# Attention with normalized queries and keys on one core: norm factors as bf16 pairs, query copies added up as 64-bit integers on GpSimd, and a new order of all engines

## The chip, the core and the metric

The kernel runs on one core of a Trainium2 chip. The core has TensorE (matrix products, into PSUM), VectorE, ScalarE and GpSimd (element-wise work), and SyncE, which here issues most DMAs. Each engine works through its own list of instructions in order; semaphores hold an instruction until its inputs are there. The metric is device time in microseconds (us) of one execution. In the profile PE is TensorE, DVE is VectorE, ACT is ScalarE, POOL is GpSimd and SP is SyncE.

## The reference

```python
B, H, S, D = 1, 32, 2048, 640
Dh = D // H          # 20
# q, k, v: [1, 32, 2048, 20] bf16;  t: [32] bf16, 1.0 and a little more
def reference(q, k, v, t):
    eps = 1e-6
    qn = q / (jnp.sqrt((q * q).sum(axis=-1, keepdims=True)) + eps)
    kn = k / (jnp.sqrt((k * k).sum(axis=-1, keepdims=True)) + eps)
    logits = jnp.einsum('bhqd,bhkd->bhqk', qn, kn) * t[None, :, None, None]
    attn = _softmax(logits, axis=-1)
    return jnp.einsum('bhqk,bhkd->bhqd', attn, v)
```

There are 32 heads with 2048 queries and 2048 keys of 20 numbers each. So the products are small and the 32 x 2048 x 2048 exponentials are many. Logits lie within about plus and minus t, so no maximum is subtracted.

## The kernel before, in words

**Preparation.** Heads are prepared in groups of one to four. VectorE squares q and k (L1008), sums over the 20 numbers (L1011), takes the reciprocal root by an integer estimate and a polynomial step (L1015 to L1030, tiles `rs_u`, `rs_a`, `rs_b`, `rs_y`, `rs_r`, all f32), multiplies the factors of the queries by the temperature of the head (L1036, `t_f`), and multiplies q and k by their factors into `qkn`, bf16, 32 columns a row (L1054). Columns 20 to 22 hold constants that make room for offsets in the products. A transposing DMA on SyncE's queue turns `qkn` into `qkT` (L1072): 32 partitions for each of four groups of rows, queries in columns 0 to 511 and keys in 512 to 1023. Six more DMAs make copies of the keys rotated among the partition groups (`kR`), four make copies of the queries with zeros in half of the partitions (`qz`). Head 0 has a shorter way of its own through TensorE (`first_head`).

**Two ways to an exponential.** A head is cut into 16 tiles of (4 x 128 keys) x 512 queries, four units of 128 x 512 each. A tile takes one of two ways.

- *ScalarE's way.* TensorE forms the query products (L1161, or L1168 with `qz`) in waves of two and three units alternately in `psA`, and ScalarE writes the exponential of a wave (1024 or 1536 columns) into `p_ring` (L1267). TensorE's value products of four units follow (L1189, `psF<-p_ring,vaug`).
- *VectorE's way.* TensorE multiplies the keys by `qP`, a copy of the queries in which each partition has been multiplied by a factor of its own (L1064, factors in `pcol`): 1 for the odd groups, 8192 for the even, and special factors on the constants. So one f32 in `psF` carries the logits of two units. VectorE reads a tile of 128 x 1024 out of `psF` as int32 with one multiplication and addition (L1318): each 32-bit word of `xt` is then two 16-bit floats, which approximate two powers of two. Three phase additions make three copies `ss` with an integer added to each word, which moves the kinks of the approximation. The additions of a tile may run on VectorE in a fast form (L1340, or two tiles in one by L1345) or a slow form with gaps in the output (L1338, only the third phase), or on GpSimd as 64-bit integer additions, two words an element, in pieces of any length (L1350). TensorE's value products read `xt` and the three `ss`, the latter with values scaled to the phase (`vph`, L971).

`DVE_TILES` lists how many of the 16 tiles of each head go VectorE's way. The list's sum is 205; ScalarE has the other 307 tiles, which are 1228 units.

**Output.** The value products of a head add up in one bank of `psF`, two banks alternating. VectorE transposes it (L1205), takes the reciprocal of the sums (L1214), multiplies (L1222), and SyncE stores two heads at a time.

**The order.** `Program.list_schedule` plans all engines before anything is issued: a list scheduler in which each task has planned duration, dependences and a due time. ScalarE's and VectorE's product tasks go ahead of value products. Each stretch of 10 us of planned time has its own set of knobs, packed in a number of `STAGES` and unpacked by `turn`. GpSimd gets its pieces in `cont_fill`. It works beside VectorE's "light" tasks (tile reads, slow phase additions, transposes); a piece is planned to begin after the last other ("heavy") VectorE task, and gets a wait on that task. Heavy tasks are the squares, sums, normalizations, query copies, fast phase additions and the like. `plan_waits` then turns dependences into semaphore waits, and `emit` writes each engine's list. Where TensorE would stand idle long, the planner may put in fillers, value products with zero weights (L1094).

The tasks around the change: `add_prep` (norms and normalization), `add_qp` (query copies; they are due 1.5 heads ahead of their head and wait for the transposing DMA of it), `add_trn` (transposes and copies by DMA), `add_wave`, `add_group` and `add_dgroup` (products, exponentials, tile reads and phase additions).

Of the kernel before, what the change touches and what calls it, by code (L numbers as in the profile page):

```python
# [10 lines left out]
BF16 = mybir.dt.bfloat16  # L11
# [42 lines left out]

class Task:
# [3 lines left out]
                 "own", "left")  # L59

    def __init__(self, eng, name, fn, dur, deps, pri, lat=0.0, dma=None):
# [13 lines left out]
        self.own, self.left = None, False  # L75
# [6 lines left out]
class Program:  # L82
# [27 lines left out]
        "WAITH": (0.3, 0.1, 0.6), "BLOG": (5, 3, 4, 7, 9, 99), "PTWO": (1, 0), "STAY": (1, 0), "URGE": (3, 2, 4, 6), "BOOST": (1.0, 0.0, 0.4, 4.0), "DPV": (0.0, 0.3, 0.65, 1.0), "FLIP": (0, 2, 4, 8), "FSOON": (0.3, 0.0, 0.8, 3.0), "JOIN": (0.8, 0.0, 0.4, 1.4), "MERGE": (0.0, 0.2, 0.4), "SLOT": (1, 0), "SPARE": (0.35, 0.25, 0.5)}  # L110
    STAGES = (323660128748544, 350903769007104, 596268605500308, 596320203303492, 596320191857220, 596316966994500, 595491402138182, 595491402132374, 595542999852948, 598645317787860, 598851709001940, 506388444610260, 258353002618204, 258353002618192, 258359452343632, 258359401581952, 258352951607584, 99844499194144, 258352951607728, 311189460894448, 311189460894448, 411357472924204, 411357472920723, 411718657544787, 570227109956499, 570220481072019, 570220481072019, 570220481072019, 543802405669779, 385293952981107, 385293941037173, 384468376180877, 701485281505421, 701485281505409, 701485818747507, 701485818802224, 701485818802224, 701472943240944, 701472943240944, 701472943239216, 859981395652608, 859981397145600, 861013771243971, 543686861512754, 543686861512752, 493378820286042, 652663031351901, 810344306477949, 648540582288375, 14500321833210, 122546067191103, 702972302468002, 24310418509344, 681779003975634, 731275100514633, 324749016460711, 324749016460711, 324749016460711, 324749016460711)
# [42 lines left out]
    def list_schedule(self, until=None):  # L154
# [166 lines left out]
        def cont_fill(now):  # L321

            n = 0
            while free["POOL"] <= now + 1e-9:
# [14 lines left out]
                fit = [r for r in ready["POOL"] if r[2].win]  # L339
                if fit:  # L340
# [3 lines left out]
                    t = x[2]  # L344
                else:
# [1108 lines left out]
```

## Time and profile before

| what | before |
|---|---|
| median of 3 runs | 572.65 us |
| lowest and highest run | 571.52 and 572.72 us |
| span of the profiled execution | 570.9 us |
| TensorE products, busy | 552.1 us (97%), 6257 instructions |
| VectorE, busy | 554.1 us (97%), 669 instructions |
| ScalarE, busy | 558.9 us (98%), 499 instructions |
| GpSimd, busy | 454.9 us (80%), 459 instructions |

The profiled execution's own time is its span, 570.9 us; the times of the runs are device times that also take in what lies around the span, and their median is 1.75 us above it. Busy time is the time in which at least one instruction of an engine has a record open. Records of neighbouring instructions may overlap, so the mean of a group of instructions can be longer than what one more of them costs. A row of the groups gives line, engine, operation, output and input, shapes, count, then busy time, mean of one in ns, and the idle time of the engine just before them with what ended it. A row of the chain of waits or of the timeline gives start, length, and what ran.

### The profile page before, as it was taken

To read this page: it belongs to the slowest core of one execution; us is meant where nothing else is said; L and a number is where in the kernel's file an instruction comes from. 1 tells how busy PE (TensorE), PEld (TensorE's weight loads), DVE (VectorE), ACT (ScalarE), POOL (GpSimd) and SP (SyncE) were. 2 spreads that over 40 slices of the span, in tenths; PEclk is the share of its full clock that TensorE was granted. 3 is DMA by queue.
4 is the path that set the end of the run, shared out by engine and by line. 5 is a ranking of instruction groups with operands and counts; after the bars stand their busy time and mean duration, and the time that the engine had idled before them with its cause. 6 is when DMAs were issued, how large, how long until landed. Compare 5 with 4: busy or idle time off the path is not lost.

```text
span 570.9 us, 15004 instructions
## 1 busy us (share of the span) xinstructions
PE 552.1 (97%) x6257; PEld 151.5 (27%) x6257; DVE 554.1 (97%) x669; ACT 558.9 (98%) x499; POOL 454.9 (80%) x459
## 2 busy tenths in 40 slices
PE   8998999999998999999999999999999999999997
PEld 2222222222222222222222222222222222222222
DVE  8999999999999999999999999999999999999994
ACT  6999999999999999999999999999999999999995
POOL 6476959687796787977989788886888969899873
PEclk9999999999999999999999999999999999999999
DMA  5553444634446433434423433434334322321000
GB/s 69 64 84 71 59 53 96 76 85 45 79 77 71 83 69 66 63 53 75 67 70 56 76 57 64 67 65 75 48 71 73 59 69 48 54 62 40 14 1 18
DMA packets 195763, 35.60 MB, mean 62 GB/s; under 512 B 172272, under 2 KB 195696, under 8 KB 195696
## 3 DMA queue, kind: packets, MB, share of 16 engines
q1 hardware_dynamic: 195552, 34.57, 37.6%
q8 instruction: 49, 0.80, 0.6%
q14 instruction: 18, 0.15, 0.1%
q10 hardware_dynamic: 144, 0.08, 0.1%
HBM read 7.87 MB, written 2.62 MB: 18 GB/s over the span
## 4 chain that ended last, share of the span: by engine, by line
ACT 80%; PE 17%; DMA 1%; DVE 1%; SPq 0%; issue 0%
ACT p_ring L1267 80%; PE psF L1189 10%; PE psA L1161 3%; PE psA L1168 2%; PE psF L1173 1%; DMA qkT<-qkn 1%; PE psF L1087 1%; SPq L844 0%; DVE xt L1318 0%; DVE oT L1205 0%; DVE ones L847 0%; DVE o_stage L1222 0%; PE psA L1121 0%; DVE qkT L1133 0%; DVE qP L1064 0%
## 5 line engine op out<-in xcount | busy, mean ns | idle before, releaser
L1267 ACT ACTIVATE p_ring<-psA 128x1024 bf16<-128x1024 f32 x492 | 555.3, 1458 | 1.6 <-PE psA L1161 1.6
L1350 POOL INT64_ADD ss<-xt x400 | 446.0, 1136 | 106.8 <-DVE qkn L1054 25.5
L1318 DVE TENSOR_SCALAR xt<-psF 128x1024 int32<-128x1024 f32 x205 | 249.1, 1215 | 2.7 <-PE psF L1173 2.3
L1189 PE MATMUL psF<-ss,vph 128*32 128x512 f16 (+1 forms) x2460 | 214.0, 397 | 0.1
L1338 DVE TENSOR_SCALAR ss<-xt 128x1040 int32<-128x1040 int32 x159 | 193.8, 1222 | 0.9 <-PE psF L1189 0.8
L1189 PE MATMUL psF<-p_ring,vaug 128*32 128x512 bf16 x1228 | 114.3, 384 | 0.4 <-DVE xt L1318 0.4
L1161 PE MATMUL psA<-qkT,kR 32*128 32x512 bf16 x655 | 100.5, 385 | 6.3 <-ACT p_ring L1267 5.1
L1189 PE MATMUL psF<-xt,vaug 128*32 128x512 bf16 (+1 forms) x820 | 82.4, 394 | 0.6 <-DVE xt L1318 0.5
L1189 PEld LDWEIGHTS psF<-ss,vph 128*32 128x32 f16 x2460 | 54.6, 94 | 81.0 <-issue 51.9
L1168 PE MATMUL psA<-qz,kR 64*128 64x512 bf16 x313 | 64.6, 386 | 1.6 <-ACT p_ring L1267 1.1
L1173 PE MATMUL psF<-qP,kR 64*128 64x512 bf16 x284 | 54.7, 382 | 1.5 <-DVE xt L1318 1.4
L1161 PEld LDWEIGHTS psA<-qkT,kR 32*128 32x128 bf16 x655 | 24.7, 91 | 100.6 <-ACT p_ring L1267 99.9
L1189 PEld LDWEIGHTS psF<-p_ring,vaug 128*32 128x32 bf16 x1228 | 30.4, 94 | 49.7 <-issue 40.1
L1161 PE MATMUL psA<-qkT 32*128 32x512 bf16 x177 | 35.1, 384 | 3.0 <-ACT p_ring L1267 2.5
L1168 PEld LDWEIGHTS psA<-qz,kR 64*128 64x128 bf16 x313 | 15.8, 92 | 63.6 <-ACT p_ring L1267 62.5
L1205 DVE STREAM_TRANSPOSE oT<-psF 128x512 f32<-128x512 f32 x32 | 22.7, 710 | 6.9 <-PE psF L1189 6.6
L1189 PEld LDWEIGHTS psF<-xt,vaug 128*32 128x32 bf16 x820 | 21.2, 94 | 30.0 <-issue 22.7
L1173 PE MATMUL psF<-qP,qkT 64*128 64x512 bf16 x126 | 24.3, 382 | 0.0
L1054 DVE TENSOR_TENSOR qkn<-qk_sb,rs_r 128x1280 bf16<-128x1280 bf16 (+1 forms) x17 | 23.2, 1362 | 0.0
L1011 DVE TENSOR_REDUCE rs_sum<-sq 128x64 f32<-128x1280 bf16 (+1 forms) x17 | 23.0, 1354 | 0.0
L1173 PEld LDWEIGHTS psF<-qP,kR 64*128 64x128 bf16 x284 | 13.7, 93 | 24.1 <-DVE xt L1318 11.3
L1168 PE MATMUL psA<-qz,qkT 64*128 64x512 bf16 x83 | 19.8, 386 | 0.1
(75 smaller groups left out, 144.0 us busy)
## 6 DMA issues: line engine op xcount, KB each, us to landing
kR<-qkT SPq DMA_DIRECT2D x62, 96.0 KB, 2.2
kR<-qkT SPq DMA_DIRECT2D x62, 64.0 KB, 2.1
qz<-qkT SPq DMA_DIRECT2D x104, 32.0 KB, 1.9
qk_sb<-in_k_dram SPq DMA_DIRECT2D x32, 80.0 KB, 3.0
vaug<-in_v_dram SPq DMA_DIRECT2D x32, 80.0 KB, 3.3
qk_sb<-in_q_dram SPq DMA_DIRECT2D x124, 20.0 KB, 2.5
out_dram<-o_stage SPq DMA_DIRECT2D x31, 80.0 KB, 1.8
kR<-qkT SPq DMA_DIRECT2D x62, 32.0 KB, 1.9
```

The source lines that it names most:

```text
L1011: sums.append(dv("sum", lambda e, tk, i=i, m2=m2, src=src: e.tensor_reduce(rs["sum"][:, 2 * R * i:2 * R * i + m2], src, AXIS_X, ALU.add), ...
L1054: norm[h] = [dv("norm", lambda e, tk, x=x, b=b, i=i, m=m: e.tensor_tensor(qkn_all[:, b:b + m, :, :].rearrange("p n r w -> p (n r) w")[:, : ...
L1087: warm.append(add("PE", "warm", lambda e, tk: e.matmul(psO[0], ones[:, 0:128], ones[:, :], start=True, stop=True), PE_MM, [z_one], -300))
L1161: return eng.matmul(dst, k_of(h, c, (rho - g) % 4, ps), qkT[h % NT][ps, 0:512], tile_position=(32 * g, 0))
L1168: return eng.matmul(dst, k_of(h, c, (rho - g) % 4, ps), qz[h % NZ][ps, g % 2, :], tile_position=(64 * b, 0))
L1173: return eng.matmul(dst, k_of(h, c, dl, ps), qP[h % NT][ps, :], tile_position=(64 * b, 0))
L1189: last = eng.matmul(psO[h % 2][32 * g:32 * g + 32, :], w_of(g), rhs_of(g), start=start, stop=False, skip_group_check=True, tile_position=( ...
L1205: trO[h] = add("DVE", f"tr{h}", lambda e, tk: e.transpose(oT_all[:, so, :, :].rearrange("p r d -> p (r d)"), psO[h % 2]), 0.63, [lambda: p ...
L1267: act[w] = add("ACT", f"exp{w}", lambda e, tk: e.activation(p_ring[:, p0 * 512:p0 * 512 + n], psA[:, slot * WAVES[0] * 512:slot * WAVES[0] ...
L1318: return add("DVE", name, lambda e, tk: e.tensor_scalar(dst[:, o + 2 * w0:o + 2 * (w0 + n)].bitcast(I32), psF[:, prog.pair_of[j] + w0:prog ...
L1338: return e.tensor_scalar(gapped(be).bitcast(I32)[:, :, 0:PAD], xt[0][:, bx:bx + TILE].bitcast(I32), float(PHASE_W[i]), None, ALU.add)
L1350: f.alt = lambda c, n, i=i, dst=dst, be=be: lambda e, tk: e.int64_add(dst[:, be + 2 * c:be + 2 * (c + n)].bitcast(I64), xt[0][:, bx + 2 * ...
```

## The change

**Norm factors as pairs.** The factors stay f32 up to `rs_r`. One multiplication then writes `r2`, a bf16 tile with every factor twice side by side, already multiplied by the temperature for the queries and by one for the keys; `t2` holds temperature and one. The normalization reads q and k as ten pairs a row and the pair of factors ten times over, so that all its operands are bf16. Head 0 keeps its own way.

**Query copies on GpSimd.** For heads 1 to 31, `qP` is no longer a product on VectorE but a 64-bit integer addition on GpSimd. Each 64-bit element is four bf16 numbers; adding 13 to an exponent field multiplies by 8192. `pbits` holds what is to be added in each partition, including differences of bit patterns for the constants. It is built once by one memset and 13 selects on GpSimd. In `cont_fill` a copy takes its place among the pieces.

**Tiles and order.** `DVE_TILES` adds up to 207, so that ScalarE has 305 tiles, 1220 units. Planned durations, two knobs, `STAGES`, and with them the order on all engines, are new.

The instruction counts of the two orders, where they differ in number (counts of the order, in which a piece or an instruction is one):

| engine, instruction | before | after |
|---|---|---|
| ScalarE exponentials of 1536, 1024, 512 columns | 245, 246, 1 | 244, 244, 0 |
| VectorE tile reads (L1318) | 205 | 207 |
| VectorE phase additions, slow (L1338), fast (L1340), fast of two (L1345) | 159, 9, 2 | 162, 15, 2 |
| VectorE query copies (L1064) | 32 | 1 |
| VectorE products of norms and temperatures (L1036) | 11 | 11, four times the elements |
| GpSimd phase additions (L1350), 32-bit words in them | 400, 454,768 | 342, 452,608 |
| GpSimd query copies of 256 words | 0 | 31 |
| TensorE value products on `ss`, `xt`, `p_ring` | 2460, 820, 1228 | 2484, 828, 1220 |
| TensorE fillers (L1094) | 80 | 28 |
| TensorE products behind the last query product | 60 | 36 |

SyncE's DMAs are the same in kind and number, in another order.

```diff
+def bits(x):
+    b, = struct.unpack("<I", struct.pack("<f", x))
+    return b + 0x7FFF + (b >> 16 & 1) >> 16
+def from_bits(b):
+    return struct.unpack("<f", struct.pack("<I", b << 16))[0]
...
@@ cont_fill
-                fit = [r for r in ready["POOL"] if r[2].win]
+                fit = [r for r in ready["POOL"] if r[2].win and (r[2].parent or not drain or at + r[2].win <= free["DVE"] + self.OVER)]
...
+                    if not t.parent:
+                        t.trig = d[k] if k >= 0 else None
+                        t.start, t.end = at, at + t.win
+                        free["POOL"] = lock[0] = t.end
+                        order["POOL"].append(t)
...
-                        x = min(two) if two and min(two)[0] < x[0] + 0.3 else x
+                        x = min(two) if two and min(two)[0] < x[0] + self.PNEAR else x
+                        if self.PSKIP and not two and len(cand) > len(fast):
+                            x = min(r for r in cand if r[2].sdur)
@@ list_schedule
+                    if t.gap is not None and t.gap.slow:
+                        t.end += 0.016
@@ constants
-    PE_MM = 0.227
+    PE_MM, PE_QK, PE_PV = 0.227, 0.216, 0.223
-    DVE_TILES = [5, 6, 6, 7, 6, 7, 6, 7, 6, 7, 6, 7, 6, 7, 6, 7, 7, 6, 7, 6, 7, 6, 7, 6, 7, 6, 7, 6, 7, 7, 6, 5]
+    DVE_TILES = [5, 6, 6, 7, 6, 7, 7, 6, 7, 6, 7, 7, 6, 7, 7, 6, 7, 6, 7, 7, 6, 7, 7, 6, 7, 6, 7, 7, 6, 7, 6, 5]
-    EXP0 = 0.063
+    EXP0 = 0.0635
+    QP_DUR = 0.5
@@ tiles
-        t_f32 = sbuf("t_f32", [128, H], F32)
+        t2 = sbuf("t2", [128, H, 2], F32)
+        pbits = sbuf("pbits", [128, 4], BF16)
+        r2_all = sbuf("r2", [128, 2 * NQ * R, 2], BF16)
@@ start
+        zb = [add("POOL", "z", lambda e, tk: e.memset(pbits[:, :], 0.0), 0.06, [], -60.0)]
+        def fill_bits(cols, base, op, val):
+            zb.append(add("POOL", "z", lambda e, tk: e.affine_select(
+                pbits[:, cols], pbits[:, cols], [[0, cols.stop - cols.start]], op, val, base=base, channel_multiplier=1),
+                0.15, [zb[-1]], -59.9 + 0.01 * len(zb)))
+        for g, val in ((3, from_bits(13 << 7)), (2, 0.0), (1, from_bits(13 << 7))):
+            fill_bits(slice(0, 4), -32 * g, ALU.is_ge, val)
...
+        z_t2 = add("DVE", "z", lambda e, tk: e.memset(t2[:, :, 1:2], 1.0), 0.1, [], -96.85)
@@ add_prep
+        def wide(o, n):
+            a = r2_all[:, o:o + n, :]
+            return bass.AP(a.tensor, a.offset, [a.ap[0], [2, n], [0, D // 2], [1, 2]])
-                f = lambda e, tk: e.tensor_tensor(rq, rq, tq, ALU.mult)
+            c = dv("rs", lambda e, tk: e.tensor_tensor(
+                r2_all[:, 0:w, :].rearrange("p (m r) z -> p m r z", r=R),
+                bass.AP(r.tensor, r.offset, [r.ap[0], [R, 2 * n], [1, R], [0, 2]]),
+                bass.AP(tk2.tensor, tk2.offset, [tk2.ap[0], [1, 2 * n], [0, R], [0, 2]]), ALU.mult), 0.07 + 0.066 * n, [c, tcp, z_t2])
...
-                    qkn_all[:, b:b + m, :, :].rearrange("p n r w -> p (n r) w")[:, :, 0:D], x,
-                    bc(rs["r"][:, 2 * R * i:2 * R * (i + m)], 2 * R * m), ALU.mult), 0.067 + 0.667 * m, [c] + war, i)]
+                    qkn_all[:, b:b + m, :, :].rearrange("p n r (w z) -> p (n r) w z", z=2)[:, :, 0:D // 2, :],
+                    x.rearrange("p r (w z) -> p r w z", z=2), wide(2 * R * i, 2 * R * m), ALU.mult), 0.067 + 0.3335 * m, [c] + war, i)]
@@ add_qp
-            qp[h] = add("DVE", f"qp{h}", lambda e, tk: e.tensor_scalar(
-                qP[h % NT][:, :], qkT[h % NT][:, 0:512], pcol[:, 0:1], None, ALU.mult),
-                0.262, deps + zc[-1:] + ([lambda: qk_users[h - NT]] if h >= NT else []), h - QLEAD if h else -26.1)
+            qp[h] = add("POOL", f"qp{h}", lambda e, tk: e.int64_add(
+                qP[h % NT][:, :].bitcast(I64), qkT[h % NT][:, 0:512].bitcast(I64), pbits[:, :].bitcast(I64).to_broadcast([128, 128])),
+                QP_DUR, deps + [zb[-1]] + ([lambda: qk_users[h - NT]] if h >= NT else []), h - QLEAD)
+            qp[h].win = QP_DUR
```

The new numbers of `STAGES` are left out; `t2` takes the place of `t_f32` where ScalarE writes it and where head 0 reads it.

More of the change, by code (lines that the diff above doesn't have):

```diff
@@ L58 @@
                  "alt", "parts", "parent", "rem", "glue", "room", "next", "head", "wide", "slow", "sdur", "pair", "base", "two", "need",
-                 "own", "left")
+                 "own", "left", "gap")
     def __init__(self, eng, name, fn, dur, deps, pri, lat=0.0, dma=None):
@@ L74, in __init__ @@
         self.need = None
-        self.own, self.left = None, False
+        self.own, self.left, self.gap = None, False, None
 Wake = Task("DVE", "wake", None, 0.0, [], 0.0)
@@ L344, in cont_fill @@
                     t = x[2]
+                    if not t.parent:
[3 more added lines that the diff above has]
+                        order["POOL"].append(t)
+                        heapq.heappush(events, (t.end, 1, t.seq, t))
+                        leave(t, now)
+                        n += 1
+                        continue
                 else:
```

53 lines of the change are left out of this document (34 added, 19 removed).

## The prediction

> **What bounds the kernel now.** I read the busy shares, then the stretches, the chain of waits, and the groups by shape.
>
> ```profile
> span 570.9 us, 15004 instructions
> PE 552.1 (97%) x6257; PEld 151.5 (27%) x6257; DVE 554.1 (97%) x669; ACT 558.9 (98%) x499; POOL 454.9 (80%) x459
> PEclk9999999999999999999999999999999999999999
> ...
> core 0: us, PE busy (x) PEld busy (x) DVE busy (x) ACT busy (x) POOL busy (x), PEclk, DMA share, GB/s
> 220.00:260.00 40.00, 39.01 (x446) 10.26 (x443) 39.83 (x51) 40.00 (x37) 31.92 (x30) 1.00 0.40 71
> 460.00:500.00 40.00, 39.21 (x464) 10.80 (x456) 39.81 (x43) 40.00 (x37) 33.74 (x30) 1.00 0.31 60
> ```
>
> Three engines are full at once, GpSimd nearly so, and the granted clock is 1.00. The chain says which one sets the end:
>
> ```profile
> ACT 80%; PE 17%; DMA 1%; DVE 1%; SPq 0%; issue 0%
> ...
> 8.26 158.31 ACT p_ring L1267 x140
> 169.79 4.88 DMA qkT<-qkn
> 177.55 299.78 ACT p_ring L1267 x265
> 563.79 3.53 PE psF L1189 x53
> ```
>
> ScalarE's exponentials run from 8.26 us on, one behind the other: 265 of them in 299.78 us is 1.131 us each, 2.262 a pair. After the last of them comes a piece of TensorE alone. So the span is: start, number of exponentials times their pace, ScalarE's gaps, and a tail. VectorE and GpSimd matter where they hold TensorE up.
>
> **The change part by part.** Counts are from the two instruction orders.
>
> *ScalarE.* 207 VectorE tiles in place of 205 leave 1220 units of 512 columns for 1228.
>
> ```profile
> L1267 ACT ACTIVATE p_ring<-psA 128x1536 bf16<-128x1536 f32 x245 | 409.3, 1671 | 1.0 <-PE psA L1161 1.0
> L1267 ACT ACTIVATE p_ring<-psA 128x1024 bf16<-128x1024 f32 x246 | 307.1, 1248 | 0.6 <-PE psA L1161 0.6
> L1267 ACT ACTIVATE p_ring<-psA 128x512 bf16<-128x512 f32 x1 | 0.8, 758 | 0.0
> ```
>
> The new order has 244 of 1536, 244 of 1024 and none of 512. The records overlap (409.3 + 307.1 exceeds the span), so I price by differences: 1671 - 1248 = 423 ns for 512 columns, and (2.262 - 5 x 0.423) / 2 = 0.073 us fixed. Eight units fewer are 8 x 0.423 = 3.4 us, four instructions fewer 0.3: **-3.7 us**, on the path. If TensorE, not ScalarE, set the pace, this would be 0; taken whole, since ScalarE is 40.00 of 40 in the stretches.
>
> *The tail.*
>
> ```profile
> 551.59 13.02 ACT L1267 ACTIVATE p_ring<-psA 128x1024 bf16<-128x1024 f32 x12
> 566.01 1.28 PE L1189 MATMUL psF<-p_ring,vaug 128*32 128x512 bf16 x20
> 567.34 0.72 DVE L1205 STREAM_TRANSPOSE oT<-psF 128x512 f32<-128x512 f32 x1 [5.94 <-PE psF L1189]
> ```
>
> The last exponential ends at 564.61, yet TensorE works until 567.31: 2.7 us of backlog. Behind the last query product the old order has 60 value products (fifteen groups of four in 3.53 us, 0.235 a group), the new one 36: 9 x 0.235 = 2.1 us. The last exponential there is one of 1536, whose record takes 1.67 us, and one group must follow it: at least 1.67 + 0.24 = 1.9. So TensorE ends about 0.4 us behind the last exponential, not 2.7. The gain lies between 2.3 and 0 (a backlog that comes with the last product late); I take **-2.0 us**, because both countings nearly meet. What follows (567.31 to 570.9) is unchanged.
>
> *Gaps of ScalarE.* The one visible gap:
>
> ```profile
> 174.69 0.35 DVE L1064 TENSOR_SCALAR qP<-qkT,pcol 128x512 bf16<-128x512 bf16 x1 [1.16 <-DMA qkT<-qkn]
> 177.55 2.37 ACT L1267 ACTIVATE p_ring<-psA 128x1536 bf16<-128x1536 f32 x2 [1.03 <-PE psA L1161]
> ```
>
> VectorE stood at a query copy until its transposing DMA landed; the tile reads behind it, then TensorE's query products, then ScalarE came late. In the new order this copy stands on GpSimd, where the tile reads are not queued. The same DMA late would now hold up the phase additions behind the copy. Gap gone is -1.0, a gap like it in a new place 0: **-0.5 us**, the middle, for the order is new everywhere.
>
> *Start.* One more VectorE memset, of the constants beside the temperatures, in the unbroken run before head 0.
>
> ```profile
> 2.08 0.09 DVE L889 MEMSET p_ring<- 128x32 bf16 x1
> L910 POOL TENSOR_SCALAR_AFFINE_SELECT pcol<-pcol 128x1 bf16<-128x1 bf16 x12 | 2.3, 193 | 0.0
> L1350 POOL INT64_ADD ss<-xt x400: 371/1040/1922, 18.1 to 561.5; - x134
> ```
>
> **+0.1 us.** GpSimd gets one memset and 13 selects (2.6 us) behind its old start-up work; its first phase addition is at 18.1 us, so they lie in idle time. Uncovered they would delay only head 1's copy.
>
> *VectorE.*
>
> ```profile
> L1318 DVE TENSOR_SCALAR xt<-psF 128x1024 int32<-128x1024 f32 x205 | 249.1, 1215 | 2.7 <-PE psF L1173 2.3
> L1338 DVE TENSOR_SCALAR ss<-xt 128x1040 int32<-128x1040 int32 x159 | 193.8, 1222 | 0.9 <-PE psF L1189 0.8
> L1205 DVE STREAM_TRANSPOSE oT<-psF 128x512 f32<-128x512 f32 x32 | 22.7, 710 | 6.9 <-PE psF L1189 6.6
> L1340 DVE TENSOR_SCALAR ss<-xt 128x1024 int32<-128x1024 int32 x9 | 6.6, 736 | 0.0
> L1064 DVE TENSOR_SCALAR qP<-qkT,pcol 128x512 bf16<-128x512 bf16 x32 | 12.3, 389 | 1.2 <-DMA qkT<-qkn 1.2
> L1054 DVE TENSOR_TENSOR qkn<-qk_sb,rs_r 128x1280 bf16<-128x1280 bf16 x14 | 20.7, 1479 | 0.0
> L1054 DVE TENSOR_TENSOR qkn<-qk_sb,rs_r 128x640 bf16<-128x640 bf16 x3 | 2.4, 816 | 0.0
> L1008 DVE TENSOR_TENSOR sq<-qk_sb 128x1280 bf16<-128x1280 bf16 x14 | 12.0, 860 | 0.0
> L1008 DVE TENSOR_TENSOR sq<-qk_sb 128x640 bf16<-128x640 bf16 x3 | 1.4, 482 | 0.0
> L1036 DVE TENSOR_TENSOR rs_r<-rs_r,t_f 128x64 f32<-128x64 f32 x5 | 1.1, 225 | 0.2
> L1027 DVE SCALAR_TENSOR_TENSOR rs_y<-rs_b 128x128 f32<-128x128 f32 x5 | 1.4, 283 | 0.0
> ```
>
> Added: 2 tile reads (2.4), 3 slow phase additions (3.7), 6 fast ones (4.4). Removed: 31 query copies (-12.1). The 17 normalizations multiply bf16 by f32 now and cost 1479 and 816 ns; the squares, bf16 by bf16 on the same sizes, cost 860 and 482. With norms as bf16 pairs both factors are bf16: 14 x 0.62 + 3 x 0.33 = -9.7. Bounds: 0, if reading one pair ten times does not count as dense, and -9.7; I take the squares' price, nearest in size, type and operation. The product of norms with temperatures writes four times the elements (256 for 64): 283 - 225 = 58 ns for 64 elements gives some 0.4 us for 256, at most +0.2 for each of 11, +1.4 at the most 2.2. Sum: 10.5 - 12.1 - 9.7 + 1.4 = **about -9.9 us** on 554.1, off the path while VectorE stays under ScalarE's pace. It pays for the two tiles in a span six us shorter; without it VectorE would need 554 us in about 565, less the 6 us it waits at the end.
>
> The Trainium skill, "VectorE: DVE Perf Modes", What auto-detection actually checks, gives the doubled rate to 16-bit operands with steps of one; its innermost step is one here, which by that rule leads to the squares' price. No run shows the repeated pair yet.
>
> *GpSimd.*
>
> ```profile
> L1350 POOL INT64_ADD ss<-xt x400 | 446.0, 1136 | 106.8 <-DVE qkn L1054 25.5 <-DVE rs_r L1036 19.1 <-DVE sq L1008 14.6
> qkT<-qkn SPq DMA_TRANSPOSE x31, 3.1
> ```
>
> Phase additions go from 400 instructions with 454,768 words to 342 with 452,608. 371 ns (the shortest, 224 words) and 1040 (1024 words) give 0.84 ns a word and 0.18 us fixed: 58 x 0.18 + 2160 x 0.84 ns = -12.5 us. Added are 31 copies of 256 words with a second tensor read. At the one-tensor line one is 0.4 us; twice the shortest row is 0.74. I take 0.5, nearer the row of its size: +15.5. Net +3, +5.6 with the selects. Room: GpSimd is busy 454.9 and held while VectorE does its other work (554.1 - 249.1 - 193.8 - 22.7 = 88.5): 27.5 us free. Afterwards it is held 88.5 - 12.1 - 9.7 + 1.4 + 4.4 = 72.5 and busy 445.1 + 31c, c a copy's whole stay at the queue's head: in 564.8 us that leaves 47 - 31c, 31.7 us at c = 0.5. Behind a copy are queued phase additions, and behind those TensorE's value products.
>
> The Trainium skill, "GPSIMD Engine Reference", 3.1, speaks against it: two tensors share a read port, some 2.6 cycles an element. By it a copy is an estimated 0.55 + 0.18 = 0.74 us and GpSimd's net +10.4 us; the time stays, as 24 us remain free.
>
> *TensorE.* Value products: +24 for VectorE tiles, +8 of their reads, -8 of ScalarE's: six groups, +1.4 us; four waves of query products less and two tile products more, -0.5; fillers without work 80 to 28, 13 groups, -3.1.
>
> ```profile
> L1094 PE MATMUL psF<-ones,nil 128*32 128x512 bf16 x80 | 6.7, 385 | 0.0
> ```
>
> About -2 us, off the path but for the tail.
>
> **Sum.** -3.7 - 2.0 - 0.5 + 0.1 = -6.1 us: span 570.9 to 564.8. The median of the runs, 572.65, lies 1.75 above the profiled span (the runs 0.6 to 1.8), which I add: **566.5 us**.
>
> **The rivals.** (1) *The new order stalls more.* ScalarE has 0.2 us of slack a stretch on VectorE (39.83 of 40), and an order fixed for 570 us meets DMAs that land at other times, as at 174.69. Two to four such gaps of 1.03 us more and half the tail kept give 566.5 + 2 to 4 + 1 = 569.5 to 571.5. For it: every wait is in a new place. Against: only one such gap now, and VectorE's load falls.
> (2) *The pairs change nothing*: normalizations stay at 1479 ns. VectorE then has the old 554 us to do in 565; a shortage of 5 to 6 us lands on the tile reads: 572, no change. Against it: the squares' row.
> (3) *The copies block GpSimd*, which ends slower. When c passes 47 / 31 = 1.5 us, GpSimd is the bound; the time is 566.5 + 31(c - 1.5), and over 572.65 from c = 1.7. At c = 2, half of the 3.1 us that a transpose takes to land plus 0.5, it is 582. For it: a queue in order, and a wait on a DMA at its head. Against: one copy in 32 waited now (1.2 us in all), as copies come well behind their transposes.
>
> **How the numbers follow.** Forecast 0.60 (564 to 569), rival 1 0.20, rival 2 0.06, rival 3 0.14. Range: low 563.5, the forecast with the full gap (-0.5) and tail (-0.3) gained, the runs' lowest offset (0.6 for 1.75) and 2 ns off the pace (488 x 0.002 = 1.0), since 1.131 holds small waits that no row lists; high 572.5, with rivals 1 and 2 inside and rival 3 out; the likeliest case's own is 564 to 569. No change means within 0.2% (1.1 us), about what can be told. Faster: 0.60 + 0.19 = 0.79; same: 0.01 + 0.05 = 0.06; slower: 0.14 + 0.01 = 0.15.
>
> **What would show it.** Right: 488 exponentials at 1.131 us; TensorE's last value product within 1 us of the last exponential; normalizations near 860 ns; copies under 0.8 us; VectorE busy near 544. Wrong: ScalarE idle before its line by over 4 us; additions on GpSimd waiting for the transposing DMA or products waiting for GpSimd by far more; a granted clock under 1.00 now that fillers are gone.

## The result, and the profile after

The changed kernel takes 566.1 us (median of 4 runs, 565.9 to 566.7) against 572.66 us for the kernel before beside it: a ratio of 0.989, with a 95% interval of 0.988 to 0.990. The forecast was 566.5. The profiled execution's span is 564.5 us, 1.7 below the 566.2 that the device time of the same execution gives; so span and device time are two measures, as far apart here as the 1.75 us that were added for the forecast.

Line numbers have moved: the exponentials are L1324 now (before L1267), tile reads L1375 (L1318), slow and fast phase additions on VectorE L1395 and L1397 (L1338, L1340), phase additions on GpSimd L1407 (L1350), value products L1246 (L1189), query products L1218, L1225 and L1230 (L1161, L1168, L1173), normalization L1106 (L1054), squares L1058 (L1008), query copies L1120 (L1064). The top of the page, and two stretches by engine:

```profile
span 564.5 us, 14903 instructions
PE 546.8 (97%) x6225; PEld 149.6 (27%) x6225; DVE 547.7 (97%) x650; ACT 555.3 (98%) x495; POOL 467.8 (83%) x446
PEclk9999999999999999999999999999999999999999
...
220.00:260.00 40.00, 39.97 (x476) 11.11 (x472) 39.51 (x40) 40.00 (x36) 37.88 (x27) 1.00 0.52 80
460.00:500.00 40.00, 39.65 (x456) 10.78 (x455) 39.77 (x46) 40.00 (x37) 34.30 (x30) 1.00 0.28 53
```

ScalarE is still busy 40.00 of 40 us and the granted clock is still 1.00. GpSimd alone has more to do (467.8 us for 454.9). The chain of waits, and the end of the timeline:

```profile
ACT 80%; DVE 10%; PE 9%; issue 0%; DVEq 0%
...
8.47 114.03 ACT p_ring L1324 x101
...
185.87 335.94 ACT p_ring L1324 x297
...
558.71 2.16 PE psF L1246 x31
```

```profile
547.15 13.19 ACT L1324 ACTIVATE p_ring<-psA 128x1536 bf16<-128x1536 f32 x11
...
559.78 1.06 PE L1246 MATMUL psF<-p_ring,vaug 128*32 128x512 bf16 x16
...
560.89 0.72 DVE L1262 STREAM_TRANSPOSE oT<-psF 128x512 f32<-128x512 f32 x1 [5.35 <-PE psF L1246]
```

The long piece of exponentials runs at the pace of before: 335.94 / 297 = 1.131 us each. The last one ends at 560.34, and TensorE at 560.84, 0.5 us later; before, it was 2.7 us. The chain's DVE pieces, 10% that were 1% before, lie between 126 and 185 us, where VectorE's reads and additions stand back to back just as ScalarE's exponentials do; the list of ScalarE's waits has nothing there, and ScalarE is busy for 40.00 of the 40 us from 140 to 180. So the two engines are about level there. The groups that the change touches:

```profile
L1324 ACT ACTIVATE p_ring<-psA 128x1536 bf16<-128x1536 f32 x244 | 400.1, 1640 | 0.1
L1324 ACT ACTIVATE p_ring<-psA 128x1024 bf16<-128x1024 f32 x244 | 297.8, 1220 | 0.6 <-PE psA L1218 0.6
...
L1375 DVE TENSOR_SCALAR xt<-psF 128x1024 int32<-128x1024 f32 x207 | 251.6, 1215 | 2.4 <-PE psF L1230 1.9
L1395 DVE TENSOR_SCALAR ss<-xt 128x1040 int32<-128x1040 int32 x162 | 197.2, 1222 | 0.6 <-PE psF L1246 0.3
L1058 DVE TENSOR_TENSOR sq<-qk_sb 128x1280 bf16<-128x1280 bf16 x14 | 11.6, 832 | 0.0
L1106 DVE TENSOR_TENSOR qkn<-qk_sb,r 128x1280 bf16<-128x1280 bf16 x14 | 11.2, 811 | 0.0
L1397 DVE TENSOR_SCALAR ss<-xt 128x1024 int32<-128x1024 int32 x15 | 10.4, 693 | 0.0
L1090 DVE TENSOR_TENSOR r<-rs_r,t 128x256 bf16<-128x256 f32 x5 | 2.1, 425 | 0.2
L1106 DVE TENSOR_TENSOR qkn<-qk_sb,r 128x640 bf16<-128x640 bf16 x3 | 1.5, 488 | 0.0
```

```profile
L1407 POOL INT64_ADD ss<-xt x342 | 436.6, 1294 | 83.8 <-DVE sq L1058 20.6 <-DVE r L1090 14.4 <-DVE qkn L1106 13.9
L1120 POOL INT64_ADD qP<-qkT,pbits x31 | 19.4, 626 | 4.6 <-DVE o_stage L1279 1.9 <-DVE sq L1058 1.8 <-DVE xt L1375 0.9
L942 POOL TENSOR_SCALAR_AFFINE_SELECT pbits<-pbits 128x4 bf16<-128x4 bf16 (+2 forms) x13 | 4.1, 319 | 1.7
```

The normalization costs what the squares cost, and ScalarE's listed idle time before the exponentials is 0.7 us where it was 1.6. A query copy on GpSimd takes 0.63 us, a little over the 0.5 assumed. None of the 4.6 us that GpSimd waited at the copies' turn is put down to a DMA.

Where the 6.4 us of span went:

| piece | before | after | difference |
|---|---|---|---|
| first exponential starts | 8.26 | 8.47 | +0.2 |
| first exponential to the end of the last | 556.35 | 551.87 | -4.5 |
| from there to the end of TensorE | 2.70 | 0.50 | -2.2 |
| from there to the end of the span | 3.6 | 3.66 | +0.1 |

### The profile page after: what moved, and what is told of

Read it like the earlier page. It is cut to its first block, busy times and chain, and to the rows that moved or that the text cites. A ratio compares the mean times of both kernels' runs of the same rounds, so it can differ in the third digit from the quotient of the medians.

```text
span 564.5 us, 14903 instructions
## 1 busy us (share of the span) xinstructions
PE 546.8 (97%) x6225; PEld 149.6 (27%) x6225; DVE 547.7 (97%) x650; ACT 555.3 (98%) x495; POOL 467.8 (83%) x446
## 4 chain that ended last, share of the span: by engine, by line
ACT 80%; DVE 10%; PE 9%; issue 0%; DVEq 0%
ACT p_ring L1324 80%; PE psF L1246 5%; DVE xt L1375 4%; DVE ss L1395 4%; PE psA L1218 1%; PE psA L1225 1%; PE psF L1144 1%; PE psF L1230 1%; DVE rs_sum L1061 0%; DVE oT L1262 0%; DVE vph L1021 0%; DVE qkn L1106 0%; DVE sq L1058 0%; PE psA L1178 0%; DVE rec L1271 0%
## 5 line engine op out<-in xcount | busy, mean ns | idle before, releaser
L1324 ACT ACTIVATE p_ring<-psA 128x1024 bf16<-128x1024 f32 x488 | 551.8, 1430 | 0.7 <-PE psA L1218 0.6
L1407 POOL INT64_ADD ss<-xt x342 | 436.6, 1294 | 83.8 <-DVE sq L1058 20.6
L1375 DVE TENSOR_SCALAR xt<-psF 128x1024 int32<-128x1024 f32 x207 | 251.6, 1215 | 2.4 <-PE psF L1230 1.9
L1246 PE MATMUL psF<-ss,vph 128*32 128x512 f16 (+1 forms) x2484 | 217.2, 397 | 0.6 <-DVE xt L1375 0.5
L1395 DVE TENSOR_SCALAR ss<-xt 128x1040 int32<-128x1040 int32 x162 | 197.2, 1222 | 0.6 <-PE psF L1246 0.3
L1246 PE MATMUL psF<-p_ring,vaug 128*32 128x512 bf16 x1220 | 109.5, 383 | 0.6 <-DVE xt L1375 0.6
L1218 PE MATMUL psA<-qkT,kR 32*128 32x512 bf16 x649 | 99.0, 385 | 5.7 <-ACT p_ring L1324 4.6
L1246 PE MATMUL psF<-xt,vaug 128*32 128x512 bf16 (+1 forms) x828 | 81.8, 393 | 0.0
L1246 PEld LDWEIGHTS psF<-ss,vph 128*32 128x32 f16 x2484 | 53.0, 94 | 92.8 <-issue 64.5
L1225 PE MATMUL psA<-qz,kR 64*128 64x512 bf16 x311 | 64.6, 386 | 2.5 <-ACT p_ring L1324 1.9
L1230 PE MATMUL psF<-qP,kR 64*128 64x512 bf16 x288 | 55.5, 382 | 0.9 <-DVE xt L1375 0.6
L1218 PEld LDWEIGHTS psA<-qkT,kR 32*128 32x128 bf16 x649 | 24.3, 91 | 98.9 <-ACT p_ring L1324 96.4
L1246 PEld LDWEIGHTS psF<-p_ring,vaug 128*32 128x32 bf16 x1220 | 29.1, 94 | 40.2 <-issue 29.9
L1218 PE MATMUL psA<-qkT 32*128 32x512 bf16 x179 | 34.3, 384 | 1.7 <-ACT p_ring L1324 1.0
L1225 PEld LDWEIGHTS psA<-qz,kR 64*128 64x128 bf16 x311 | 15.8, 92 | 62.6 <-ACT p_ring L1324 61.2
L1246 PEld LDWEIGHTS psF<-xt,vaug 128*32 128x32 bf16 x828 | 21.1, 94 | 28.7 <-issue 21.5
L1230 PE MATMUL psF<-qP,qkT 64*128 64x512 bf16 x126 | 24.3, 382 | 0.4 <-POOL qP L1120 0.2
L1120 POOL INT64_ADD qP<-qkT,pbits x31 | 19.4, 626 | 4.6 <-DVE o_stage L1279 1.9
L1230 PEld LDWEIGHTS psF<-qP,kR 64*128 64x128 bf16 x288 | 13.9, 93 | 25.2 <-DVE xt L1375 12.8
L1225 PE MATMUL psA<-qz,qkT 64*128 64x512 bf16 x81 | 19.8, 386 | 0.2 <-ACT p_ring L1324 0.2
```

The source lines that it names most:

```text
L1120: qp[h] = add("POOL", f"qp{h}", lambda e, tk: e.int64_add(qP[h % NT][:, :].bitcast(I64), qkT[h % NT][:, 0:512].bitcast(I64), pbits[:, :].b ...
L1218: return eng.matmul(dst, k_of(h, c, (rho - g) % 4, ps), qkT[h % NT][ps, 0:512], tile_position=(32 * g, 0))
L1225: return eng.matmul(dst, k_of(h, c, (rho - g) % 4, ps), qz[h % NZ][ps, g % 2, :], tile_position=(64 * b, 0))
L1230: return eng.matmul(dst, k_of(h, c, dl, ps), qP[h % NT][ps, :], tile_position=(64 * b, 0))
L1246: last = eng.matmul(psO[h % 2][32 * g:32 * g + 32, :], w_of(g), rhs_of(g), start=start, stop=False, skip_group_check=True, tile_position=( ...
L1324: act[w] = add("ACT", f"exp{w}", lambda e, tk: e.activation(p_ring[:, p0 * 512:p0 * 512 + n], psA[:, slot * WAVES[0] * 512:slot * WAVES[0] ...
```

## The experiments

All runs stand beside the kernel before, whose median was 572.5 to 572.7 in each comparison; differences to the changed kernel are against its 566.1 us. It was not run again beside them, so a difference of about a microsecond rests on the kernel before having been as steady as that.

### Are the pairs needed, and are they enough

One edit takes the pairs' effect out of the changed kernel: the factors stay doubled but become f32, with the order of every engine the same.

```diff
-        r2_all = sbuf("r2", [128, 2 * NQ * R, 2], BF16)
+        r2_all = sbuf("r2", [128, 2 * NQ * R, 2], F32)
```

> The changed kernel with the pairs of norm factors held as f32 and not bf16; the order of all engines stays as it is. Theory (ScalarE's row of exponentials sets the end, and the VectorE time freed by the bf16 pairs is what lets two more tiles through): the normalizations go back from 811 to about 1479 ns, VectorE gets 14 x 0.67 + 3 x 0.33 = 10.4 us more work, against some 4 us that it idles between start and end now, so 4 to 8 us slower than the changed kernel: 570 to 574 us. Rival (the gain comes from the new order as such, the pairs are not needed for it): 566 us, within 1 us of the changed kernel.

It took 573.5 us, ratio to the kernel before 1.0025 (1.0013 to 1.0036). Its chain, groups and exponentials:

```profile
DVE 39%; PE 32%; ACT 22%; POOL 3%; issue 2%; SPq 1%; DMA 1%; DVEq 0%
```

```profile
L1106 DVE TENSOR_TENSOR qkn<-qk_sb,r 128x1280 bf16<-128x1280 bf16 x14 | 20.6, 1485 | 0.0
...
L1106 DVE TENSOR_TENSOR qkn<-qk_sb,r 128x640 bf16<-128x640 bf16 x3 | 2.5, 823 | 0.0
```

```profile
L1324 ACT ACTIVATE p_ring<-psA 128x1536 bf16<-128x1536 f32 x244 | 381.8, 1565 | 4.8 <-PE psA L1218 4.3
```

The normalizations are back at before's price, VectorE is 9.6 us busier (557.3), and 7.4 us of that reach the time. The chain passes to VectorE, and ScalarE now waits 4.8 us, not 0.1, for query products. Without the pairs the whole change, in this order, gains nothing: it is 0.25% slower than before.

The other edit puts the pairs alone into the kernel before, in its own order:

```diff
+        t2 = sbuf("t2", [128, H, 2], F32)
+        r2_all = sbuf("r2", [128, 2 * NQ * R, 2], BF16)
...
-                    bc(rs["r"][:, 2 * R * i:2 * R * (i + m)], 2 * R * m), ALU.mult), 0.067 + 0.667 * m, [c] + war, i)]
+                    x.rearrange("p r (w z) -> p r w z", z=2), wide(2 * R * i, 2 * R * m), ALU.mult), 0.067 + 0.667 * m, [c] + war, i)]
```

> The kernel before with the bf16 pairs of norm factors alone, in its own order (the planned durations are left as they were; two small instructions for the constants are added on GpSimd at the start). VectorE has 14 x 0.65 + 3 x 0.33 - 1 = 9 us less. Theory (ScalarE's row sets the end): its 491 exponentials of two and three units and its tail of 60 products stay, so 571.5 to 572.7 us, at most the 1.0 us gap is gained. Rival (VectorE's 554 us were the bound): 564 to 569 us.

572.36 us, ratio 0.9994 (0.9986 to 1.0002): nothing, though VectorE's busy time fell by 7.2 us to 546.9. ScalarE keeps its share of the chain:

```profile
ACT 80%; PE 16%; DVE 2%; DMA 1%; SPq 0%; issue 0%
```

So VectorE's freed time is worth nothing by itself in the order of before. In the changed kernel the order turns it into tiles that ScalarE needn't do and a shorter tail.

### The exponentials and the tail

Here ScalarE gets less work in the order of the changed kernel: 232 of its exponentials of 1536 columns take 1504, and the last 32 columns are left out.

```diff
-            act[w] = add("ACT", f"exp{w}", lambda e, tk: e.activation(
-                p_ring[:, p0 * 512:p0 * 512 + n], psA[:, slot * WAVES[0] * 512:slot * WAVES[0] * 512 + n], ACT.Exp, scale=LN2),
+            act[w] = add("ACT", f"exp{w}", lambda e, tk, m=n - (32 if w >= 24 and n == 1536 else 0): e.activation(
+                p_ring[:, p0 * 512:p0 * 512 + m], psA[:, slot * WAVES[0] * 512:slot * WAVES[0] * 512 + m], ACT.Exp, scale=LN2),
```

> The changed kernel with 232 of the 244 exponentials of 1536 columns (those from the 25th wave on) done for 1504 columns only; the last 32 columns keep what an earlier wave left, so this part of the computation is left out. Order unchanged. ScalarE has 232 x 32 x 0.83 ns = 6.1 us less. Theory (ScalarE's pace sets the end, VectorE and TensorE close behind with some 4 us of room): 2 to 6 us faster, 560 to 564 us. Rival (VectorE and TensorE, 10 and 9% of the chain, set the pace now): 0 to 1 us, 565 to 566 us.

563.4 us: 2.7 us less, for some 6.1 us less of ScalarE's work (232 x 32 columns at 423 ns for 512). The chain changes hands at once:

```profile
DVE 42%; PE 37%; ACT 17%; issue 2%; DMA 1%; POOL 1%; DVEq 0%
```

ScalarE was the bound, but VectorE and TensorE stand less than 3 us behind it: the three are nearly level in the changed kernel. Of 6 us less for ScalarE alone under 3 come out; less for VectorE or TensorE alone was not tried.

The next edit moves six groups of value products back behind the last query product, so that 60 are there, as before, in place of 36.

```diff
+        back = [t for t in pe[:q] if t.name[:2] == "pv"][-6:]
...
+        self.order["PE"] = [t for t in pe[:q + 1] if t not in back] + back + pe[q + 1:]
```

> The changed kernel with six groups of four value products moved on TensorE from ahead of the last query product to behind it, so that 60 products stand there as in the kernel before, in place of 36; all else in place. Theory (the tail is TensorE's backlog at 0.235 us a group): 6 x 0.235 = 1.4 us, less 0.1: 567.2 to 567.5 us. Rival (the last exponential sets the tail): 566 us, no change.

567.53 us, 1.4 more. The last exponential ends at 560.47 (it was 560.34), and TensorE at 562.12, 1.3 us later than in the changed kernel:

```profile
547.29 13.18 ACT L1331 ACTIVATE p_ring<-psA 128x1536 bf16<-128x1536 f32 x11
...
561.08 1.04 PE L1253 MATMUL psF<-p_ring,vaug 128*32 128x512 bf16 x16
```

Six groups at 0.235 us are 1.4: what stands behind the last query product is paid for group by group.

### How much room GpSimd has

Five runs lengthen or shorten what GpSimd does at a copy's turn. The order of all other work is kept. The first puts a second addition of the same size, into a tile that nobody reads, behind each of the 31 copies:

```diff
+            if t.name[:2] == "qp":
+                for k in range(1):
+                    last = Task("POOL", "spare" + t.name, self.spare(int(t.name[2:])), 0.5, t.deps + [last], t.pri)
...
+        prog.spare = lambda h: lambda e, tk: e.int64_add(
+            spare[:, :].bitcast(I64), qkT[h % NT][:, 0:512].bitcast(I64), pbits[:, :].bitcast(I64).to_broadcast([128, 128]))
```

> The changed kernel with one more 64-bit addition of 256 words, into a spare tile, behind each of the 31 query copies on GpSimd: a copy's stay goes from 0.61 to about 1.2 us, GpSimd's work up by 18 us. Theory: GpSimd has 564.5 - 467.8 busy - 76 in which VectorE's heavy work holds it = 20 us free, so nearly all of it is covered: 566 to 569 us. Rival (phase additions queued behind a copy come late at TensorE at once, there is no room): 575 to 585 us.

The second puts two of twice the size (512 words) behind each copy:

```diff
-                for k in range(1):
+                for k in range(2):
...
-            spare[:, :].bitcast(I64), qkT[h % NT][:, 0:512].bitcast(I64), pbits[:, :].bitcast(I64).to_broadcast([128, 128]))
+            spare[:, :].bitcast(I64), qkT[h % NT][:, 0:1024].bitcast(I64), pbits[:, :].bitcast(I64).to_broadcast([128, 256]))
```

> The changed kernel with two more 64-bit additions of 512 words each behind every query copy, some 1.04 us each: GpSimd's work up by about 65 us, a copy's stay about 2.7 us. Theory: beyond the 20 us that GpSimd has free every us counts, 65 - 20 = 45 us slower: about 611 us, and products wait for GpSimd. By the line in the prediction, 566.1 + 31 x (2.7 - 1.5) = 603 us. Rival (GpSimd is not what the products wait for): under 580 us.

They took 576.0 us (ratio 1.007, 1.0046 to 1.0095) and 626.5 us (1.095, 1.091 to 1.099): 9.9 us for 19.1 us of added work, and 60.4 for 66.9. Both are far above what the prediction's line gives. The profiled execution of the first was the longest of its runs, 580.2 us, and it lost 4.5 us of ScalarE's time in one place, which made the first heads a suspect. That stretch, first in the changed kernel, then with the spares:

```profile
20.00:40.00 20.00, 18.73 (x207) 5.22 (x207) 19.92 (x32) 20.00 (x19) 12.73 (x14) 1.00 0.46 63
```

```profile
20.00:40.00 20.00, 18.40 (x143) 3.90 (x140) 15.29 (x25) 15.48 (x14) 10.99 (x12) 0.66 0.45 55
```

ScalarE is busy 15.48 us of 20, and TensorE has a granted clock of 0.66. So the next run leaves out the spares behind the copies of heads 1 to 3:

```diff
-                for k in range(1):
+                for k in range(1 if int(t.name[2:]) >= 4 else 0):
```

> The spare 256-word addition behind a query copy (616 ns each, as measured) stands here only behind the copies of heads 4 to 31: 28 of them, 17.2 us of GpSimd time in place of 19.1. Theory A (GpSimd's room is uneven: most of what the 31 spares cost was lost in the first heads, where TensorE starved and its granted clock fell): about 5.7 us of the 9.9 come back, so 569 to 572 us. Theory B (the cost is spread evenly, some 0.32 us for each spare wherever it stands): 566.1 + 28 x 0.32 = 574 to 576 us. The prediction's rule (20 us of room before anything is lost) would give 566 to 568.

575.3 us (ratio 1.0058, 1.0036 to 1.008; 573.9 to 578.8): the first heads were not it. That loss seems to belong to one execution: the other seven runs were 2 to 5 us shorter. 17.2 us of work cost 9.2 (7.8 in the shortest run), 0.28 to 0.33 us for each spare of 0.62, where the 31 spares cost 0.32 each, so it looks spread over the heads. Two last runs go down and up by a third of that. One does only the first half of the copies of heads 4 to 31 and leaves out the other, the other run adds spares of 16 words:

```diff
-            qp[h] = add("POOL", f"qp{h}", lambda e, tk: e.int64_add(
-                qP[h % NT][:, :].bitcast(I64), qkT[h % NT][:, 0:512].bitcast(I64), pbits[:, :].bitcast(I64).to_broadcast([128, 128])),
+            qp[h] = add("POOL", f"qp{h}", lambda e, tk, m=64 if h > NT else 128: e.int64_add(
+                qP[h % NT][:, 0:4 * m].bitcast(I64), qkT[h % NT][:, 0:4 * m].bitcast(I64), pbits[:, :].bitcast(I64).to_broadcast([128, m])),
```

> In the changed kernel the copies of heads 4 to 31 make only the first half of their columns (128 words in place of 256; the other half of the copy keeps an older head's values, so that part of the computation is left out). By the fixed part and the slope of the two sizes seen (613 ns at 256 words, 1.04 us at 512) a copy falls to about 0.40 us: 28 x 0.21 = 6 us of GpSimd time less, in the same order. Theory A (each microsecond on GpSimd at these places costs 0.45 us of the time, in both directions, as 17.2 us more cost 7.8): 566.1 - 2.7 = 563 to 564 us. Theory B (in the kernel as it stands the copies are covered, and only longer ones come out): 565.5 to 566.7 us, no change.

```diff
-            spare[:, :].bitcast(I64), qkT[h % NT][:, 0:512].bitcast(I64), pbits[:, :].bitcast(I64).to_broadcast([128, 128]))
+            spare[:, 0:32].bitcast(I64), qkT[h % NT][:, 0:32].bitcast(I64), pbits[:, :].bitcast(I64).to_broadcast([128, 8]))
```

> A spare addition of only 16 words behind each of the 31 copies, by the same two sizes about 0.2 us: some 6 us of GpSimd time more, in the same order. Theory A (every microsecond at these places costs 0.45 us): 568.5 to 569.5 us. Theory B (a threshold: about 0.2 us behind a copy is still covered, and the loss of 0.28 us for each 0.62 us spare lies above it): 566 to 567 us.

The halved copies took 566.4 us (565.8 to 570.6), no different from 566.1: what was cut off them had been covered, theory B. The small spares took 567.4 us (567.2 to 567.9), 1.3 more: between the two theories, nearer to a threshold. Together the runs suggest a bent line:

| run | GpSimd work at the copies | time against 566.1 | idle before the phase additions (83.8 in the changed kernel) |
|---|---|---|---|
| copies halved | -6.0 us | +0.3 | 89.3 |
| spares of 16 words | +6.8 | +1.3 | 79.4 |
| spares of 256 words, heads 4 to 31 | +17.2 | +9.2 | 74.1 |
| spares of 256 words, all | +19.1 | +9.9 | 77.4 (the execution of 580.2) |
| two spares of 512 words | +66.9 | +60.4 | 70.7 |

Between 6.8 and 19.1 us of added work a microsecond costs 0.70 ((9.9 - 1.3) / 12.3), and drawn back with that slope the cost begins at 6.8 - 1.3 / 0.70 = 4.9 us: some 5 us of room, 0.16 us for each copy. That is an estimate by two straight pieces; these runs can't tell them from a curve. The last column says where the room is not. GpSimd stands idle for 84 us before its phase additions, yet 66.9 us more work uses only 13 of them (83.8 - 70.7). Who pays is in the waits of TensorE's value products for phase additions (time in total, times, longest), in the changed kernel, with the small spares, with the late ones and with the large ones:

```profile
PEld psF L1246 <- POOL ss L1407: 7.6, 25, 0.5
```

```profile
PEld psF L1258 <- POOL ss L1419: 12.0, 39, 0.9
```

```profile
PEld psF L1258 <- POOL ss L1419: 19.3, 47, 1.6
```

```profile
PEld psF L1258 <- POOL ss L1419: 56.6, 61, 4.4
```

### What the order is worth

Here the changed kernel's work is planned with the old numbers of `STAGES`:

```diff
-    STAGES = (323660128748544, 543686867484722, 596274517665444, 3554637424947329, 1652484935479344, ...
+    STAGES = (323660128748544, 350903769007104, 596268605500308, 596320203303492, 596320191857220, ...
```

> The changed kernel planned with the old numbers of STAGES: pairs, copies on GpSimd and 207 tiles stay, the order of all engines is another. ScalarE has the same 488 exponentials. Theory: the 3.7 us of fewer exponentials stay, what is lost is in gaps of ScalarE and in the tail: 568 to 574 us. If the order had no part in the gain: 566 us.

580.8 us, ratio 1.015 (1.013 to 1.017). And here its query copies go back to VectorE, with all engines planned anew by the new numbers:

```diff
-            qp[h] = add("POOL", f"qp{h}", lambda e, tk: e.int64_add(
-                qP[h % NT][:, :].bitcast(I64), qkT[h % NT][:, 0:512].bitcast(I64), pbits[:, :].bitcast(I64).to_broadcast([128, 128])),
-                QP_DUR, deps + [zb[-1]] + ([lambda: qk_users[h - NT]] if h >= NT else []), h - QLEAD)
-            qp[h].win = QP_DUR
+            qp[h] = add("DVE", f"qp{h}", lambda e, tk: e.tensor_scalar(
+                qP[h % NT][:, :], qkT[h % NT][:, 0:512], pcol[:, 0:1], None, ALU.mult),
+                0.262, deps + zc[-1:] + ([lambda: qk_users[h - NT]] if h >= NT else []), h - QLEAD)
```

> The changed kernel with the query copies back on VectorE (one part undone); planned anew with the new knobs, which were not set for it. VectorE has 31 x 0.26 = 8 us more, GpSimd 19 us less. Theory (VectorE's time is what the copies buy): ScalarE's exponentials stay 488 but it waits more, 569 to 575 us, more than the run with the old knobs. Rival (the copies could have stayed): 566 to 568 us.

584.3 us, ratio 1.02 (1.0186 to 1.0215), above both expectations, and above the run with the old numbers. In both runs ScalarE waits for something that the changed kernel's list of waits doesn't hold: value products (L1246 and L1245) that come late, so that places in `p_ring` aren't free.

```profile
ACT p_ring L1324 <- PE psF L1246: 8.0, 7, 1.7
```

```profile
ACT p_ring L1323 <- PE psF L1245: 12.7, 9, 2.1
```

Is it the work that loses there, or the misfit of work and numbers? The control is the kernel before with nothing changed in its code but the new numbers. It has two knobs fewer, so what the numbers say of those two is not used:

```diff
-    STAGES = (323660128748544, 350903769007104, 596268605500308, 596320203303492, 596320191857220, ...
+    STAGES = (323660128748544, 543686867484722, 596274517665444, 3554637424947329, 1652484935479344, ...
```

> The kernel before, with its own work on every engine, but the order planned with the numbers (STAGES) of the changed kernel: a control for the two runs in which the changed kernel's work was planned with numbers that were fitted to other work (580.8 with the old numbers, 584.3 with the copies back on VectorE). Theory A (what those two lost is mostly the misfit between numbers and work, whatever the work): this loses 8 to 15 us too, 580 to 588 us. Theory B (the numbers matter little, and the changed kernel's own work is what lost there): 572 to 576 us.

596.7 us, ratio 1.043 (1.040 to 1.045), with the same wait:

```profile
ACT p_ring L1267 <- PE psF L1189: 14.2, 9, 6.8
```

The misfit by itself costs 24 us here, more than theory A gave. It is not made of waits alone. The order also decides which engine does a phase addition, and all three misfit orders give VectorE more slow ones, here with the old numbers, with the copies back, and in the control:

```profile
L1395 DVE TENSOR_SCALAR ss<-xt 128x1040 int32<-128x1040 int32 x182 | 221.5, 1224 | 0.8
```

```profile
L1394 DVE TENSOR_SCALAR ss<-xt 128x1040 int32<-128x1040 int32 x169 | 206.3, 1225 | 3.1 <-PE psF L1245 1.8
```

```profile
L1338 DVE TENSOR_SCALAR ss<-xt 128x1040 int32<-128x1040 int32 x176 | 214.2, 1224 | 1.5
```

The changed kernel has 162 of them, the kernel before 159. VectorE is busy for 564.6 and 563.9 us in the first two (547.7 in the changed kernel) and for 576.6 us in the control (554.1 before), which by itself is more than the kernel before takes. How much of the loss is that work and how much the late value products was not separated. So these runs tell that the new order fits its own work and no other that was tried, but not what the copies' move is worth: with 24 us of misfit to be had, 18 can't be split. What GpSimd's copies save in an order fitted to copies on VectorE stays open.

## Why the prediction was right, point by point

**The bound.** Right. ScalarE's row of exponentials set the end before and sets it after, at 1.131 us each; taking 6.1 us from ScalarE moved the time by 2.7, and in the kernel before taking 7.2 from VectorE alone did not move it.

**Exponentials and gaps.** Predicted -3.7 for the work and -0.5 for the gap at 177.55, together -4.2; measured -4.5 from the first exponential's start to the last one's end. The 244 pairs at 2.262 us are 551.9, so of the measured 551.87 nothing but the pace is left. The gap is gone and no other of its kind came: ScalarE's listed idle time fell by 0.9 us, from 1.6 to 0.7, so this term lay near its better end. Rival 1 had two to four new gaps of 1 us; there was none.

**Tail.** Predicted -2.0, measured -2.2: TensorE ends 0.5 us behind the last exponential, where 0.4 was worked out. The price of 0.235 us a group stood the test when six groups were put back.

**Start.** Predicted +0.1, measured +0.2. The first exponential's start is not steady to a tenth: with the same instructions ahead of it, it was at 8.47 in the changed kernel's profile and at 8.3 in others.

**VectorE's sum.** The mechanism was right and the sum too large: -9.9 predicted, 554.1 - 547.7 = -6.4 measured. The pairs are as forecast, 811 and 488 ns for the squares' 860 and 482, and the product of norms with temperatures 425 ns for some 0.4 us. The mis-sized term is the 31 query copies at 389 ns: that is the mean length of a record, and the next instruction starts before it ends, as here in the kernel before:

```profile
172.45 0.35 DVE L1064 TENSOR_SCALAR qP<-qkT,pcol 128x512 bf16<-128x512 bf16 x1
172.72 0.82 DVE L1008 TENSOR_TENSOR sq<-qk_sb 128x1280 bf16<-128x1280 bf16 x1
```

Most copies are followed after 0.26 or 0.27 us, one after 0.76 and one after 1.13; from start to next start the 31 add up to 9.4 us and not 12.1. With that the sum would be -7.2. The remaining 0.8 is of the size of small growth in other groups: the 15 divisions of outputs (L1279) alone went from 826 to 902 ns, 1.1 us. It cost nothing, because VectorE had a few microseconds in hand: 9.6 us more on it cost 7.4.

The Trainium skill, "VectorE: DVE Perf Modes", What auto-detection actually checks, ties the doubled rate to 16-bit operands with steps of one. The trace agrees for the pair that is read ten times over: 811 ns with bf16 factors, 1485 with f32 factors in the same layout.

**GpSimd.** Here the prediction failed in size twice, once without effect and once in its rule. A copy took 0.63 us where 0.5 was taken, inside its bounds of 0.4 and 0.74. The phase additions fell by 9.4 us for 12.5, and the 13 selects took 4.1 us for 2.6, as the two on 128 x 3 took 0.87 us each. Busy time rose by 12.9 us, not 5.6. The copies' part of it did not reach the time, as halving them showed.

The Trainium skill, "GPSIMD Engine Reference", 3.1, gives 2.6 cycles an element for two tensors, from which 0.74 us a copy was estimated, with a 32-bit word taken as an element. The measured 0.61 (median) lies between that and the 0.5 taken. That two tensors are dearer than one is borne out: 1.66 ns a word against 0.84.

The step that was wrong is the room, "in 564.8 us that leaves 47 - 31c", with GpSimd the bound from c = 1.5 us on. The runs put the bend at about 0.61 + 0.16 = 0.8 us, and the slope beyond it at 0.7 and then near 1. With two large spares a copy's turn lasts 0.61 + 2.16 = 2.8 us; the prediction's line gives 566.5 + 31 x 1.27 = 606, and 626 was measured. The failing step is that every idle microsecond of the span in which VectorE's heavy work does not hold GpSimd was counted as room. In the changed kernel's profile GpSimd is idle for 96.7 us. The largest of its waits:

```profile
POOL ss L1407 <- DVE sq L1058: 20.6, 12, 6.1
POOL ss L1407 <- DVE r L1090: 14.4, 9, 2.4
POOL ss L1407 <- DVE qkn L1106: 13.9, 10, 3.5
POOL ss L1407 <- DVE o_stage L1279: 10.2, 8, 2.2
POOL ss L1407 <- DVE vph L1021: 9.3, 9, 1.8
```

With the smaller ones 76.0 us before the phase additions end with a heavy instruction of VectorE, near the 72.5 that the prediction had taken off. Of the other 20.7 us, 5.8 lie behind the last addition, which ends at 558.69, and 7.1 at the start, the selects and the copies. So 7.8 us are left among the additions, where the prediction's line had 28 (47 less 31 copies of 0.61) and where the runs found some 5. A phase addition that came later showed as a longer wait of value products, 12.0, 19.3 and 56.6 us for 7.6. Rival 3 had the right mechanism and too late a point of decision. By this estimate the copies as built end 0.2 us short of it, so that the forecast of no loss held by a margin of some 5 us of work was in part luck.

**TensorE.** About -2 us of busy time predicted, -5.3 measured. The fillers fell from 6.7 to 2.4 us where -3.1 was expected. Off the path, as said; and the granted clock stayed at 1.00 without them.

**The rivals.** The pairs changed something, so rival 2 is out, and the run with f32 factors put its price at 573.5, where 572 had been given. The new order did not stall, yet the prediction was thin at this point. It had no way to tell a fitted order from an unfitted one by the profile of before, and the three unfitted ones lost 15 to 24 us (two against the changed kernel, the control against the kernel before), far more than the 3 to 5 of rival 1. That the order would not stall was given a chance, not worked out.

## What to carry to other kernels

Price a tuned pipeline from the row that is full, here the exponentials at their pace plus start and tail, and check what the other engines can give up at the places where they are needed, since an engine's idle time over the span is no room: of 84 us idle before GpSimd's additions, an estimated 5 were free. Freed time on an engine that isn't the bound paid here only through an order fitted to it, and the order fitted to one set of costs lost up to 4% with another, in which it also moved work from one engine to another. The cost of one more instruction is read from start to next start, not from a record's length.

## What the runs showed that was not expected

The 64-bit addition of two tensors on GpSimd took 217, 403, 614 and 1041 ns for 16, 128, 256 and 512 32-bit words: 0.19 us and 1.66 ns a word, a straight line over all four, and twice the slope of the form with one tensor (0.84).

The runs with long spares spread more. The changed kernel's runs lay within 0.7 us of each other at a granted clock of 0.997 to 1.00. With the late spares nine runs spread from 573.9 to 578.8 us, and those above 576 had clocks of 0.985 to 0.991. Two large spares gave 0.959 to 0.975. Long spares are not needed for it: one run with halved copies took 570.6 us at 0.988, where the other six took 565.8 to 567.1. So part of what the long spares cost may be a slower TensorE, which the prediction's line had no term for. It is the smaller part with the late spares, whose shortest run, at a clock of 1.00, still cost 7.8 us; what lowers the clock in some runs was not found.
